# Attention beside a gated feed-forward on one core: zero matmuls at the end, VectorE out of the last 24 banks, and one bank for two chunks' last gate and up tiles

## The chip, the cores and the metric

The kernel runs on one core of a Trainium2 chip. The metric is the time of one execution on the device, in microseconds; shorter is better. Times of the kernel before come from three runs and one further, profiled execution.

## The reference

For one sequence of 2048 rows of 640 numbers in bf16 the kernel computes an attention and a gated feed-forward on the same normalised input, and joins them:

```
xn  = layernorm(x)                                  # x: 2048 x 640
q, k, v = split(xn @ wqkv)                          # 32 heads of 20
s   = concat_h(softmax(q_h @ k_h.T / sqrt(20)) @ v_h) @ wo
h   = sigmoid(xn @ w_gate) * (xn @ w_up)            # 2048 x 1728
g   = silu(h @ w_down)                              # 2048 x 640
out = x + s * g
```

The scores are 32 matrices of 2048 x 2048, and each of their 134 million elements needs an exponential. 1728 is 13 tiles of 128 and one of 64.

## The kernel before, in words

**Setup.** Layer norm, the transposed input xnT and the first keys, queries and values come from an order written out by hand (ORDER). The change leaves it alone.

**Passes and banks.** The queries are cut into four chunks of 512 (qc), the heads into eight groups of four (g); a pass is one (qc, g), so there are 32. In a pass each head has 16 blocks of 128 keys. The scores of one head and one block fill one PSUM bank (128 keys x 512 queries), so a pass has 64 banks and the kernel NB = 2048. Four heads lie in the four row strips of TensorE. The last pass starts at bank LAST = 1984 and is cut into three parts of 256, 128 and 128 queries (PARTS), which end at banks 2016, 2032 and 2048; there a bank holds two or four blocks of keys of a narrower part.

**Who takes the exponential.** The scores go alternately into sets of three banks (sc0) and two banks (sc1). ScalarE turns a whole set into probabilities `p` with one instruction (L1293). VectorE takes single banks on the side, from one of two further PSUM banks ("spare" in the trace, "misc0" and "misc1" in the code): a cut at zero (`dy`, L1313) for each bank, then three polynomial steps for two banks together (`du` L1334, `du` L1338, `p` L1344), each of which may be split into two halves of 512 columns to let other VectorE work in between. `dve_bank` (L1231) decides which bank VectorE may take. TensorE then multiplies the probabilities by the values into the bank `oacc` (L1470, "PV" below). A column of ones in v gives the sum for the softmax.

**The planner.** All this is written by a loop that runs while the program is built. It keeps clocks of its own for TensorE, ScalarE and VectorE, with a cost for each kind of work, and at each step writes a set of scores, a PV batch, a step of some other job, or a zero matmul; so it fixes the order of the instructions on every engine. The other jobs, with due times in banks, are: keys, values and queries of later passes; `gateup_job` (L646) for one chunk and one tile of 128 gate and up columns (five matmuls L664 into one of the two banks, a tanh on ScalarE L671, five matmuls L677 into the other, and a product on VectorE L681 into `hT`); `down_job` (L687, matmuls L700); `out_job`, the output product of a finished chunk; and for the last chunk `part_job` (L758), which does the product of five of the eight head groups ahead, with matmuls L773, a step on VectorE L778 and a DMA that adds x (L781).

**Zero matmuls.** `zero_add` (L1441) writes a matmul with zero weights into `oacc` (L1446) or into a free bank (L1452) where the planner sees a gap, as long as the matmul time that it has counted in the last 3400 ns is under ENOUGH = 2500 ns. Each job step may say how much of its time counts; the matmuls with `pick` count nothing.

**The end.** The last pass but one is normalised on the chip by `near_job` (L834) and each part of the last pass by `last_job` (L895): the accumulator is copied out (`oev`, L794, L885 on VectorE, L887 on ScalarE for the last part), transposed by fp32 matmuls with `pick`, a 128 x 4 matrix that selects the four sums (L839, L912), inverted (`rq`, L846, L918), spread (`rb`, L850, L923), transposed back with a 128 x 128 identity (L857, L940) and multiplied (`oT`, L863, L947). Then follow the last three head groups of the output product (L902), the gate on VectorE (L988 for half a row tile, L970 for the last row tile), the sum (`ot`, L991) and a DMA to the output (L992).

Of the kernel before, what the change touches and what calls it, by code (L numbers as in the profile page):

```python
# [15 lines left out]
P = 128  # L16
PARTS = ((0, 256), (256, 128), (384, 128))
HEAD = 32
GH = 4
# [39 lines left out]
def kernel(  # L59
# [20 lines left out]
    fsz_list = [min(P, F - i * P) for i in range(NFT)]  # L80
    TT = S // P
# [31 lines left out]
    pick = const.tile([P, GH], FP32, name="pick")  # L113
# [62 lines left out]
    with tc.tile_pool(name="setup", bufs=1) as sp, \  # L176
# [181 lines left out]
        nc.gpsimd.memset(pick, 0.0)  # L358
        for j in range(GH):
            nc.gpsimd.memset(pick[32 * j:32 * j + 1, j:j + 1], 1.0)  # L360
# [8 lines left out]
    WINDOW, ENOUGH = 3400.0, 2500.0  # L369
# [274 lines left out]
    hTs, h_cells, d_cells = {}, {}, {}  # L644

    def gateup_job(c, kf):  # L646
        fsz = fsz_list[kf]
        if kf == 0 and c:
            yield "known", lambda: len(d_cells.get(c - 1, [])) == QC // P
        elif kf:  # L650
            yield "known", lambda: c in hTs
        yield "known", lambda: pe[0] > glu_t.get((c, kf), 1e18)
        hT_free = d_cells[c - 1] if c and not kf else []
        n = c * NFT + kf + WB - 1
        if n < NQC * NFT:
            load_glu(n // NFT, n % NFT)
        wg, wu = glu_w.pop((c, kf))
        if kf == 0:
            hTs[c] = glu[0].tile([P, NFT, QC], BF16, tag="hT", bufs=1, name="hT")
        hT = hTs[c]  # L660
        cols = slice(c * QC, (c + 1) * QC)
        held, psg = yield "bank",
        for kd in range(KD):
            nc.tensor.matmul(psg[0:fsz, :], lhsT=wg[:, kd, 0:fsz], rhs=xnT[:, kd, cols],  # L664
                             start=(kd == 0), stop=(kd == KD - 1))
            yield "mm", MM5
        made = {}

        def gate():
            made["t"] = wk.tile([P, QC], BF16, tag="tnh", bufs=2, name="tnh")  # L670
            nc.scalar.activation(out=made["t"][0:fsz, :], in_=psg[0:fsz, :], func=ACT.Tanh, scale=0.5)  # L671

        gated = act.add(480.0, [Cell(pe[0] + PE_OUT + 100.0), *tnh_free[-2:-1]], gate, 0, EXP_LAG)
        give_bank(held, gated)
        held, psu = yield "bank",
        for kd in range(KD):
            nc.tensor.matmul(psu[0:fsz, :], lhsT=wu[:, kd, 0:fsz], rhs=xnT[:, kd, cols],  # L677
                             start=(kd == 0), stop=(kd == KD - 1))
            yield "mm", MM5
        tnh_free.append(dve.add(600.0, [Cell(pe[0] + PE_OUT), gated, *hT_free],  # L680
                                lambda: nc.vector.scalar_tensor_tensor(  # L681
                                    out=hT[0:fsz, kf, :], in0=made["t"][0:fsz, :], scalar=1.0,
                                    in1=psu[0:fsz, :], op0=ALU.add, op1=ALU.mult), 1))
        give_bank(held, tnh_free[-1])
        h_cells.setdefault(c, []).append(tnh_free[-1])

    def down_job(tt):  # L687
# [7 lines left out]
        for h in range(2):  # L695
            e0_, e1_ = h * HALF, (h + 1) * HALF
            held, psd = yield "bank",
            for kf in range(NFT):
                fsz = fsz_list[kf]
                nc.tensor.matmul(psd[:, 0:HALF], lhsT=hT[0:fsz, kf, t4 * P:(t4 + 1) * P],  # L700
                                 rhs=glu[1][0:fsz, kf, e0_:e1_], start=(kf == 0), stop=(kf == NFT - 1))
# [56 lines left out]
    def part_job(t4):  # L758
# [5 lines left out]
        if not ahead:  # L764
            buf = glu[0].tile([P, NFT, QC], BF16, tag="hT", bufs=1, name="hT")
# [68 lines left out]
    def near_job(qc, g):  # L834
# [3 lines left out]
        for k in range(QC // P):  # L838
            nc.tensor.matmul(pd[:, k * GH:(k + 1) * GH], lhsT=oev[:, k * P:(k + 1) * P], rhs=pick,  # L839
                             start=True, stop=True, skip_group_check=True)  # L840
# [54 lines left out]
    def last_job(u):  # L895
# [15 lines left out]
        for k in range(n):  # L911
            nc.tensor.matmul(pd[:, k * GH:(k + 1) * GH], lhsT=part["oev"][:, k * P:(k + 1) * P], rhs=pick,  # L912
                             start=True, stop=True, skip_group_check=True)
            yield "mm", 250.0, 0.0

        def invert():
            made["rq"] = wk.tile([P, n, GH], FP32, tag="den", bufs=2, name="rq")
            nc.vector.reciprocal(out=made["rq"].rearrange("p t j -> p (t j)"), in_=pd[:, 0:GH * n])  # L918
# [86 lines left out]
    PART_DUE = [LAST - 8 + 8 * t4 for t4 in range(4)]  # L1005
# [39 lines left out]
    for c in range(NQC):  # L1045
# [3 lines left out]
        for kf in range(NFT):  # L1049
            jobs.append(Job(gateup_job(c, kf), GU_COST, 0, STAGE_END[c]))  # L1050
# [36 lines left out]
    def load_bulk():  # L1087
        if not glu_from or sum(bulk) == NFT + XT or front() < glu_from[0] + BULK_EVERY * (1 + sum(bulk)):
            return
        if bulk[0] < NFT:  # L1090
            kf = bulk[0]
            fsz = fsz_list[kf]
            nc.sync.dma_start(out=glu[1][0:fsz, kf, :], in_=B_w_down[kf * P:kf * P + fsz, :])
# [347 lines left out]
    def zero_add(room):  # L1441
        if streamed() >= ENOUGH or (0.0 if mode[0] == "fill" else INTO["fill"]) + MM5 > room:
# [164 lines left out]
```

## Time and profile before

| what | value |
|---|---|
| median of three runs | 887.37 us (885.86 to 888.43) |
| the profiled execution's own time | 887.83 us |
| its span, first to last instruction | 885.8 us |
| TensorE busy | 810.3 us (91%) |
| VectorE busy | 849.6 us (96%) |
| ScalarE busy | 864.0 us (98%) |
| mean granted clock of TensorE | 0.993 |

"Busy" is the time in which at least one instruction of the engine was under way. Matmuls overlap each other in the array, so TensorE's share says little by itself. All places in time below count from the first instruction of the span. In rows of the timeline the first number is the start and the second the length, both in microseconds; instructions of one kind that follow each other are merged into one row with their count.

### The profile page before, as it was taken

The numbers are of one execution on the slowest core, as the hardware profiler recorded it, in microseconds if no ns is written. First come the engines' busy times: TensorE is split into PE (matmuls) and PEld (weight loads), VectorE is DVE, ScalarE is ACT, GpSimd is POOL, SyncE is SP. The second block draws the span as 40 slices with busy tenths as digits, with TensorE's granted clock in tenths as the row PEclk, the third lists the DMA queues.
The fourth block names the chain that finished last, engine by engine and source line by source line (L and its number), as shares of the span: only waits on it lengthen the run. The fifth ranks groups of instructions, "written<-read, shape, count | busy, mean of one in ns | idle before, by whom it ended". The sixth has DMA issues, their size and how long they took to land.

```text
span 885.8 us, 16787 instructions
## 1 busy us (share of the span) xinstructions
PE 810.3 (91%) x6380; PEld 295.7 (33%) x6459; DVE 849.6 (96%) x1198; ACT 864.0 (98%) x830; POOL 158.3 (18%) x304
## 2 busy tenths in 40 slices
PE   8999999899998999999999999999999999999896
PEld 3434333332222333232233432232333332233344
DVE  7799999999999999999999999999999999999996
ACT  7999999999999999999999999999999999999994
POOL 8401111110111112111111221110112211111200
PEclk9999999999999999999999999999999999999988
DMA  8212231115542124322321243212222343200120
GB/s 319 59 52 61 73 105 36 50 53 143 154 127 58 35 82 87 56 65 66 80 50 52 80 72 79 66 41 65 54 64 66 94 67 79 64 20 14 29 46 31
DMA packets 107446, 64.10 MB, mean 72 GB/s; under 512 B 80226, under 2 KB 101750, under 8 KB 107274
## 3 DMA queue, kind: packets, MB, share of 16 engines
q1 hardware_dynamic: 97382, 47.21, 20.2%
q0 software_dynamic: 9984, 15.83, 7.9%
q8 instruction: 50, 0.82, 0.4%
q14 instruction: 30, 0.25, 0.1%
HBM read 50.18 MB, written 16.11 MB: 75 GB/s over the span
## 4 chain that ended last, share of the span: by engine, by line
ACT 50%; DVE 18%; issue 16%; PE 13%; DMA 2%; SPq 0%; POOL 0%; DVEq 0%; ACTq 0%; POOLq 0%
ACT p L1293 47%; PE sc L1267 4%; DVE dy L1313 4%; DVE du L1338 3%; DVE du L1334 3%; DVE p L1344 3%; PE work L700 2%; PE oacc L1470 2%; ACT tnh L671 2%; PE work L664 1%; DMA wqd<-in_A_wqkv_dram 1%; DVE hT L681 1%; PE oacc L1446 1%; ACT td L711 1%; PE work L677 1%
## 5 line engine op out<-in xcount | busy, mean ns | idle before, releaser
L1293 ACT ACTIVATE p<-sc 128x1536 bf16<-128x1536 f32 x711 | 818.8, 1341 | 3.2 <-PE sc L1267 1.6
L1267 PE MATMUL sc<-qT,kT_all 21*128 21x512 bf16 (+2 forms) x1889 | 278.9, 371 | 50.3 <-ACT p L1293 44.3
L1313 DVE TENSOR_SCALAR dy<-spare 128x512 f32<-128x512 f32 x271 | 184.7, 682 | 9.2 <-PE spare L1267 6.8
L1267 PEld LDWEIGHTS <-kT_all 21*128 21x128 bf16 x2176 | 90.2, 91 | 287.1 <-issue 274.9
L1334 DVE SCALAR_TENSOR_TENSOR du<-dy 128x1024 f32<-128x1024 uint16 (+1 forms) x163 | 169.0, 1038 | 2.4
L1338 DVE SCALAR_TENSOR_TENSOR du<-du,dy 128x1024 f32<-128x1024 f32 (+1 forms) x156 | 167.5, 1075 | 1.1
L1344 DVE SCALAR_TENSOR_TENSOR p<-du,dy 128x1024 uint16<-128x1024 f32 (+1 forms) x153 | 167.2, 1092 | 0.8
L1470 PE MATMUL oacc<-p,v_all 128*21 128x512 bf16 (+2 forms) x2176 | 158.1, 371 | 1.1 <-issue 0.5
L1267 PE MATMUL spare<-qT,kT_all 21*128 21x512 bf16 (+2 forms) x287 | 103.9, 373 | 1.6 <-DVE hT L681 0.7
L700 PE MATMUL work<-wd,hT 128*128 128x320 bf16 x448 | 80.3, 302 | 0.0
L798 POOL DMA_DIRECT2D den_dram<-oev x30 | 17.5, 583 | 346.9 <-DVE oev L794 307.5
L664 PE MATMUL work<-xnT,wg 128*128 128x512 bf16 (+1 forms) x263 | 75.8, 382 | 3.4 <-DVE dy L1313 1.5
L677 PE MATMUL work<-xnT,wu 128*128 128x512 bf16 (+1 forms) x263 | 73.0, 381 | 2.7 <-DVE dy L1313 0.7
L814 POOL DMA_DIRECT2D rl<-rec_dram x120 | 60.2, 523 | 54.9 <-DMA rec_dram<-den 48.4
L1470 PEld LDWEIGHTS <-v_all 128*21 128x21 bf16 x2176 | 32.2, 90 | 61.2 <-issue 57.7
L1446 PE MATMUL oacc<-xnT,zero 128*128 128x512 bf16 x140 | 48.6, 392 | 2.2 <-issue 2.2
L700 PEld LDWEIGHTS <-hT 128*128 128x128 bf16 x448 | 36.7, 97 | 41.2 <-issue 31.0
L808 POOL DMA_DIRECT2D rec_dram<-den x30 | 16.3, 545 | 134.8 <-DVE den L807 134.8
L671 ACT ACTIVATE tnh<-work 128x512 bf16<-128x512 f32 (+1 forms) x56 | 38.9, 694 | 0.0
L681 DVE SCALAR_TENSOR_TENSOR hT<-tnh,work 128x512 bf16<-128x512 bf16 (+1 forms) x56 | 37.8, 675 | 0.1
L677 PEld LDWEIGHTS <-wu 128*128 128x128 bf16 (+1 forms) x280 | 24.1, 98 | 39.0 <-issue 21.6
L664 PEld LDWEIGHTS <-wg 128*128 128x128 bf16 (+1 forms) x280 | 22.0, 98 | 40.4 <-issue 28.4
(132 smaller groups left out, 578.3 us busy)
## 6 DMA issues: line engine op xcount, KB each, us to landing
wg<-in_B_w_gate_dram SPq DMA_DIRECT2D x52, 160.0 KB
wu<-in_B_w_up_dram SPq DMA_DIRECT2D x52, 160.0 KB
rl<-rec_dram POOLq DMA_DIRECT2D x120, 64.0 KB, 2.4
qT<-q_dram SPq DMA_DIRECT2D x31, 128.0 KB
gq_dram<-d POOLq DMA_DIRECT2D x12, 320.0 KB, 2.5
gqr<-gq_dram SPq DMA_DIRECT2D x12, 320.0 KB
kT_all<-k_dram SPq DMA_DIRECT2D x28, 128.0 KB
wd<-in_B_w_down_dram SPq DMA_DIRECT2D x13, 160.0 KB
```

Source lines behind the costliest of these rows:

```text
L664: nc.tensor.matmul(psg[0:fsz, :], lhsT=wg[:, kd, 0:fsz], rhs=xnT[:, kd, cols], start=(kd == 0), stop=(kd == KD - 1))
L677: nc.tensor.matmul(psu[0:fsz, :], lhsT=wu[:, kd, 0:fsz], rhs=xnT[:, kd, cols], start=(kd == 0), stop=(kd == KD - 1))
L700: nc.tensor.matmul(psd[:, 0:HALF], lhsT=hT[0:fsz, kf, t4 * P:(t4 + 1) * P], rhs=glu[1][0:fsz, kf, e0_:e1_], start=(kf == 0), stop=(kf == N ...
L814: nc.gpsimd.dma_start(out=t["rl"][32 * j:32 * j + 32, :], in_=rec_dram[n, j:j + 1, :].to_broadcast([32, QC]))
L1267: nc.tensor.matmul(ps[:, c0:c0 + n], lhsT=kT_all[rows, g, kt * P:(kt + 1) * P], rhs=qTs[qc, g][rows, q0:q0 + n], start=True, stop=True, ti ...
L1293: nc.scalar.activation(out=buf.tile(), in_=ps, func=ACT.Exp, bias=EXP_BIAS, scale=exp_scale)
L1313: nc.vector.tensor_scalar(out=pair.y[:, i * 512:(i + 1) * 512], in0=ps, scalar1=LEAST, scalar2=None, op0=ALU.max)
L1334: nc.vector.scalar_tensor_tensor(out=t["u"][:, a:e], in0=t["f"][:, a:e], scalar=CUBE_2, in1=t["f"][:, a:e], op0=ALU.add, op1=ALU.mult)
L1338: nc.vector.scalar_tensor_tensor(out=t["u"][:, a:e], in0=t["u"][:, a:e], scalar=CUBE_1, in1=t["f"][:, a:e], op0=ALU.add, op1=ALU.mult)
L1344: nc.vector.scalar_tensor_tensor(out=t["p"][:, a:e], in0=t["u"][:, a:e], scalar=CUBE_SCALE, in1=t["y"][:, a:e], op0=ALU.mult, op1=ALU.add)
L1446: nc.tensor.matmul(oacc, lhsT=zero, rhs=xnT[:, 0, 0:QC], start=not begun, stop=not begun, skip_group_check=True)
L1470: nc.tensor.matmul(oacc[32 * j:32 * j + 1 + Dh, q0:q0 + width], lhsT=v_all[:, kt, GH * g + j, 0:1 + Dh], rhs=buf.ap[:, i, c0:c0 + width], ...
```

## The change

1. **Zeros.** From bank LAST - 16 on, the limit ENOUGH on zero matmuls is lifted: every gap that the planner sees and that is long enough gets one. After the last PV, zeros may fill the wait of the last jobs as well.
2. **The small transposes.** `pick` is gone; the transposes of `oev` use the 128 x 128 identity, and the inversion reads every 32nd column. The planner counts 200 of their 330 ns as matmul time.
3. **VectorE's share.** `dve_bank` gives VectorE none of the banks from NB - 24 on.
4. **Part products.** The `part_job`s of the last chunk are due at LAST - 24, - 16, - 8 and 0 in place of LAST - 8, 0, + 8 and + 16, and a job that waits for an event (`near_job`, `last_job`) goes to the head of the jobs under way.
5. **The 64-wide tiles.** The last gate and up tile has 64 columns. Chunks 0 and 1, and chunks 2 and 3, now do it together: for each of the five steps one matmul for the one chunk into the upper 64 rows of a bank and one for the other chunk into the lower 64, from the two halves of TensorE's columns; then one tanh and one product of 128 rows, into a tile `hE` of its own. The job count of gate and up falls from 56 to 54. The last 64 rows of w_down are loaded twice, so that both halves find them.

From the first shared tile on the planner's order differs: on ScalarE from the 283rd of its 828 instructions, on TensorE from the 4043rd of 12872.

```diff
+    EDGE = fsz_list[-1]
+    assert 2 * EDGE == P
...
-    pick = const.tile([P, GH], FP32, name="pick")
...
-    WINDOW, ENOUGH = 3400.0, 2500.0
+    WINDOW, ENOUGH, ZEROS = 3400.0, 2500.0, 16
...
     def gateup_job(c, kf):
...
+        both = kf == NFT - 1
+        if both:
+            hEs[c] = hEs[c + 1] = glu[0].tile([P, QC], BF16, tag="hE", bufs=1, name="hE")
+            fsz = 2 * EDGE
+        into = hEs[c] if both else hTs[c][:, kf, :]
+
+        def product(ps, w, kd):
+            for k in range(1 + both):
+                nc.tensor.matmul(ps[EDGE * k:EDGE * (k + 1), :] if both else ps, lhsT=w[:, kd, 0:EDGE if both else P],
+                                 rhs=xnT[:, kd, (c + k) * QC:(c + k + 1) * QC], start=(kd == 0), stop=(kd == KD - 1),
+                                 tile_position=(0, EDGE * k), skip_group_check=both)
+
         held, psg = yield "bank",
         for kd in range(KD):
-            nc.tensor.matmul(psg[0:fsz, :], lhsT=wg[:, kd, 0:fsz], rhs=xnT[:, kd, cols],
-                             start=(kd == 0), stop=(kd == KD - 1))
-            yield "mm", MM5
+            product(psg, wg, kd)
+            yield "mm", MM5 + 60.0 * both, MM5
...
     def near_job(qc, g):
...
-            nc.tensor.matmul(pd[:, k * GH:(k + 1) * GH], lhsT=oev[:, k * P:(k + 1) * P], rhs=pick,
+            nc.tensor.matmul(pd[:, k * P:(k + 1) * P], lhsT=oev[:, k * P:(k + 1) * P], rhs=identf,
                              start=True, stop=True, skip_group_check=True)
-            yield "mm", 250.0, 0.0
+            yield "mm", 330.0, 200.0
...
-            nc.vector.reciprocal(out=made["rq"].rearrange("p t j -> p (t j)"), in_=pd[:, 0:GH * QC // P])
+            nc.vector.reciprocal(out=made["rq"].rearrange("p t j -> p (t j)"), in_=pd[:, 0:QC:P // GH])
...
-    PART_DUE = [LAST - 8 + 8 * t4 for t4 in range(4)]
+    PART_DUE = [LAST-24 + 8 * t4 for t4 in range(4)]
...
-        for kf in range(NFT):
+        for kf in range(NFT - c % 2):
             jobs.append(Job(gateup_job(c, kf), GU_COST, 0, STAGE_END[c]))
...
-            flight.insert(0 if x.due >= NB else sum(y.when is not None for y in flight), x)
+            flight.insert(0, x)
...
     def dve_bank(banks):
         b = min((x for x in coming(GH) if x not in banks), default=None)
         if b is None:
+            return None
+        if b >= NB - 24:
             return None
...
     def zero_add(room):
-        if streamed() >= ENOUGH or (0.0 if mode[0] == "fill" else INTO["fill"]) + MM5 > room:
+        if streamed() >= (ENOUGH if at_bank[0] < LAST - ZEROS else 1e9) or (0.0 if mode[0] == "fill" else INTO["fill"]) + MM5 > room:
             return False
...
-    take_part(len(PARTS) - 1, pe[0])
+    oacc_free[0] = take_part(len(PARTS) - 1, pe[0])
     while flight or jobs or timed or act.queue or dve.queue:
         advance(pe[0])
         if not fill(len(steps) - 1):
-            pe[0] += 50.0
+            waits = [c.t for j in flight if j.asks and j.asks[0] == "wait" for c in j.asks[1]]
+            if not (flight or jobs) or None in waits or not zero_add(max(waits, default=1e18) - pe[0]):
+                pe[0] += 50.0
```

How many instructions of each kind the program has, before and after: exponentials on ScalarE 711 and 711, of the same sizes; tanh 56 and 54; `dy` on VectorE 271 and 271; products of gate and up on VectorE 56 and 54; polynomial steps in VectorE's queue 472 and 486, since the planner splits more of them into halves; zero matmuls in `oacc` 183 and 193.

More of the change, by code (lines that the diff above doesn't have):

```diff
@@ L911, in last_job @@
         for k in range(n):
-            nc.tensor.matmul(pd[:, k * GH:(k + 1) * GH], lhsT=part["oev"][:, k * P:(k + 1) * P], rhs=pick,
+            nc.tensor.matmul(pd[:, k * P:(k + 1) * P], lhsT=part["oev"][:, k * P:(k + 1) * P], rhs=identf,
                              start=True, stop=True, skip_group_check=True)
-            yield "mm", 250.0, 0.0
+            yield "mm", 330.0, 200.0
         def invert():
             made["rq"] = wk.tile([P, n, GH], FP32, tag="den", bufs=2, name="rq")
-            nc.vector.reciprocal(out=made["rq"].rearrange("p t j -> p (t j)"), in_=pd[:, 0:GH * n])
+            nc.vector.reciprocal(out=made["rq"].rearrange("p t j -> p (t j)"), in_=pd[:, 0:n * P:P // GH])
         def spread():
@@ L1092, in load_bulk @@
             fsz = fsz_list[kf]
-            nc.sync.dma_start(out=glu[1][0:fsz, kf, :], in_=B_w_down[kf * P:kf * P + fsz, :])
+            for r in range(0, P, fsz):
+                nc.sync.dma_start(out=glu[1][r:r + fsz, kf, :], in_=B_w_down[kf * P:kf * P + fsz, :])
             bulk[0] += 1
```

35 lines of the change are left out of this document (16 added, 19 removed).

## Prediction

> **What bounds the kernel now.** I read the chain of waits on the page first, then the costliest groups, then the busy time by windows, and last the timeline of the end.
>
> ```profile
> ACT 50%; DVE 18%; issue 16%; PE 13%; DMA 2%; SPq 0%; POOL 0%; DVEq 0%; ACTq 0%; POOLq 0%
> ...
> L1293 ACT ACTIVATE p<-sc 128x1536 bf16<-128x1536 f32 x711 | 818.8, 1341 | 3.2 <-PE sc L1267 1.6
> L1267 PE MATMUL sc<-qT,kT_all 21*128 21x512 bf16 (+2 forms) x1889 | 278.9, 371 | 50.3 <-ACT p L1293 44.3
> ```
>
> Half of the chain is ScalarE (ACT), nearly all of it the exponentials of L1293. Of TensorE's idle time ahead of scores, 44.3 us is spent waiting for ScalarE; the reverse wait is 1.6 us. So in the long middle TensorE has room, and only what takes time from ScalarE, or makes it wait, moves the end. In the windows below the first numbers are the stretch and its length, then busy time and instructions of PE, PEld, DVE, ACT and POOL, then the granted clock, the DMA share and GB/s.
>
> ```profile
> 58.00:860.00 802.00, 741.08 (x5674) 259.81 (x5744) 785.34 (x1057) 799.40 (x746) 131.23 (x238) 1.00 0.28 68
> 846.64:850.06 3.42, 2.88 (x25) 0.94 (x25) 3.42 (x5) 3.42 (x5) 0.00 (x0) 1.00 0.09 20
> 853.47:856.88 3.41, 3.15 (x51) 2.04 (x45) 3.38 (x5) 3.41 (x4) 0.00 (x0) 1.00 0.38 87
> 856.88:860.30 3.42, 3.22 (x43) 1.23 (x45) 3.42 (x6) 3.38 (x4) 0.00 (x0) 0.50 0.00 0
> 860.30:863.71 3.41, 3.08 (x32) 2.09 (x25) 2.16 (x3) 2.52 (x3) 0.00 (x0) 0.50 0.00 0
> ```
>
> From 58 to 860 us ScalarE rests 802.00 - 799.40 = 2.6 us. The end is different: from 856.88 to 863.71 TensorE has half its clock, and ScalarE is busy for only 2.52 of the last 3.41 us of it. The timeline of ScalarE's end, and of TensorE where ScalarE waits:
>
> ```profile
> 859.33 1.02 ACT L1293 ACTIVATE p<-sc 128x1024 bf16<-128x1024 f32 x1
> 860.88 2.53 ACT L1293 ACTIVATE p<-sc 128x1536 bf16<-128x1536 f32 x2 [0.53 <-PE spare L1267]
> 864.46 10.06 ACT L1293 ACTIVATE p<-sc 128x1536 bf16<-128x1536 f32 x9 [1.05 <-PE sc L1267]
> 875.23 0.28 ACT L887 ACTIVATE oev<-oacc 128x128 f32<-128x128 f32 x1 [0.71 <-PE oacc L1470]
> ```
> ```profile
> 862.60 1.37 PE L857 MATMUL work<-identf,rb 128*128 128x128 f32 x6
> 863.90 0.42 PE L1267 MATMUL sc<-qT,kT_all 21*128 21x128 bf16 x12
> ```
>
> Two stalls of 0.53 and 1.05 us, and between them and the last exponential nothing: 22 banks in 10.06 us, 0.457 us a bank. The longer stall ends with scores that stand in TensorE's queue behind six fp32 records (two for each matmul of the program), which take 1.37 us at half clock. After the last exponential (874.52) come 11.3 us in which ScalarE has one instruction. So the end has three parts: ScalarE's work, its stalls at half clock, and the closing chain.
>
> **The change part by part.**
>
> *ScalarE's work.* The exponentials stay 711, of the same sizes. Two tanh go.
>
> ```profile
> 634.01 0.66 ACT L671 ACTIVATE tnh<-work 64x512 bf16<-64x512 f32 x1
> 634.49 2.43 ACT L1293 ACTIVATE p<-sc 128x1536 bf16<-128x1536 f32 x2
> ```
>
> A tanh of 64 rows holds ScalarE for 634.49 - 634.01 = 0.48 us. Two of them: **-0.96 us**, on the engine that sets the end. Bounds: 2 x 0.66 = 1.32 at most; at least 0, if the planner's new order makes ScalarE rest that much longer.
>
> *VectorE.* Two products of gate and up go, and 14 polynomial steps more are halves.
>
> ```profile
> 849.12 1.21 DVE L1344 SCALAR_TENSOR_TENSOR p<-du,dy 128x1024 uint16<-128x1024 f32 x1
> 850.25 0.68 DVE L1313 TENSOR_SCALAR dy<-spare 128x512 f32<-128x512 f32 x1
> 850.86 0.48 DVE L778 SCALAR_TENSOR_TENSOR hT<-work,kT_all 128x320 f32<-128x320 f32 x1
> ```
>
> Start to start, 1024 columns take 1.13 us and 512 take 0.61, so a split costs 2 x 0.61 - 1.13 = 0.09 us: 14 x 0.09 = 1.3 against 2 x 0.61 = 1.2 saved. I take zero. VectorE takes 271 banks as before; within them three in place of four lie in the last part of the queries. That one bank costs ScalarE 0.46 us at the end and spares it as much earlier; while ScalarE has no rest, the place is the same to it.
>
> *The shared 64-wide tiles on TensorE.* 40 matmuls of 512 columns become 20 pairs.
>
> ```profile
> 839.64 0.61 PE L1470 MATMUL oacc<-p,v_all 128*21 128x512 bf16 x8 [0.25 <-issue]
> 856.40 0.38 PE L1446 MATMUL oacc<-xnT,zero 128*128 128x512 bf16 x1 [0.16 <-issue]
> 868.57 0.60 PE L1446 MATMUL oacc<-xnT,zero 128*128 128x512 bf16 x2
> ```
>
> A second matmul of 512 columns adds 0.60 - 0.38 = 0.22 us. Eight PV matmuls take only 0.61 us: two groups of four, side by side in strips of 32 columns. No row shows two strips of 64; the nearest is PV. If a pair goes side by side it takes 0.22 us and 20 of them save 4.4 us of TensorE; if one after the other, nothing is saved and each pair takes 0.43 us where the planner counts 0.276, 20 x 0.154 = 3.1 us too late in all. I take side by side. The 44.3 us of waiting for ScalarE cover either; without that cover the 3.1 us would go to ScalarE. The added DMA (64 rows of w_down) and four loads fewer on SP's queue I cost at nothing: the tile is needed only at the first down product, and the planner lets 4 us pass after the last of these loads.
>
> *Transposes with the identity.* Four columns become 128, and fp32.
>
> ```profile
> 854.42 0.61 PE L839 MATMUL work<-pick,oev 128*128 128x4 f32 x4
> 869.91 0.61 PE L940 MATMUL work<-identf,rb 128*128 128x128 f32 x4
> ...
> 853.47:856.88 3.41, 1.22 (x8) 1.04 (x8) 1.00 0.38 87
> ```
>
> Four records take 0.61 us with `pick` and 0.61 us with the identity, so their time is unchanged. What changes is what they do for the clock. The last row is L839 alone in the window before the clock fell: 1.22 of its 3.15 busy us are matmuls of four columns. The window at 846.64 is less busy (2.88 us), without such matmuls, and the clock stayed. So the clock follows the columns sent, not the time that a record is open. Counting 0.21 us for 512 columns and four strips as one, I get 1.1 us for 853.47 and 1.5 us for 846.64; the fall lies between. In the new order the eight records there send 128 columns, the near job starts five banks earlier, and the thinnest stretch that I find, banks 2018 to 2029, has 2.1 us of columns in ten ScalarE banks (4.6 us), 1.6 us in 3.41. I therefore expect the full clock to hold. Then the 1.05 us stall goes, whose cause is in the rows: **-1.05 us**. In the new order two of the four transposes also stand behind a set of scores. The stall of 0.53 us I leave standing as a bound.
>
> [...]
>
> *Zeros.* In the order there are 22 from bank 1968 on, 23 before. Each costs TensorE 0.22 us, or twice that at half clock, ahead of whatever the planner did not foresee. The rows 868.57 show two of them while ScalarE ran on without a rest. I cost them at nothing; bound + 0.5 us for one or two that land before late scores.
>
> *The closing chain.* Before, two PV batches and two out-products stand after the last scores; then:
>
> ```profile
> 874.55 0.63 PE L1470 MATMUL oacc<-p,v_all 128*21 128x128 bf16 x32
> 875.11 0.99 PE L902 MATMUL work<-wo_pad,oT 128*128 128x320 bf16 x6
> 878.52 0.43 PE L902 MATMUL outs<-wo_pad,oT 128*128 128x320 bf16 x2
> ...
> 876.25 0.18 DVE L918 RECIPROCAL rq<-side 128x4 f32<-128x4 f32 x1
> 876.47 0.23 DVE L923 COPY rb<-rq 128x128 f32<-128x128 f32 x1
> 877.04 0.83 DVE L991 TENSOR_TENSOR ot<-kT_all,hT 128x640 bf16<-128x640 f32 x1 [0.34 <-PE work L940]
> 877.78 0.28 DVE L947 TENSOR_TENSOR oT<-oev,work 128x128 bf16<-128x128 f32 x1
> 878.18 0.48 DVE L988 SCALAR_TENSOR_TENSOR kT_all<-work,kT_all 128x320 f32<-128x320 f32 x1
> 879.44 0.82 DVE L970 SCALAR_TENSOR_TENSOR kT_all<-outs,kT_all 128x640 f32<-128x640 f32 x1
> 881.82 0.82 DVE L991 TENSOR_TENSOR ot<-kT_all,hT 128x640 bf16<-128x640 f32 x1
> ```
>
> From the first `rq` to the last `ot` VectorE has 12 instructions here and 881.82 - 876.25 = 5.57 us. In the new order the second part is finished before the last scores' exponentials, since its scores no longer wait for VectorE, and only seven remain: rq, rb, ot, oT, ot, gate, ot. Counted from the end of the last PV (874.55 + 0.63 = 875.18 before): three out-matmuls end at 0.51, the last half gate starts at 0.55 and is 0.48 us long, `rq` starts at 1.03 (1.07 before), `rb` at 1.25, `ot` at 1.48, `oT` 0.74 later at 2.22, the second `ot` at 2.50, the gate at 3.24 (its `outs` end at 2.22 + 0.28 + 0.43 = 2.93), the last `ot` 0.82 after it at 4.06. Before, it starts at 881.82 - 875.18 = 6.64. So **-2.58 us**. It is less if half gates of the second part come late as well: one more of them and its `ot` in this chain cost 0.48 + 0.74 us, which leaves -1.4. What follows the last `ot` stays 885.80 - 881.82 us.
>
> Sum: 0.96 + 1.05 + 2.58 = 4.59 us. The profiled execution took 887.83 us, of which the span is 885.8 and 2.0 lie around it: 883.2. It lies 0.46 us above the median of the runs, 887.37, so for the median 882.8.
>
> **The rivals.**
>
> *The clock falls again (0.20).* [...] For it: I know two windows on either side of the limit, not the limit. Then the stalls stay, and 0.96 + 2.58 = 3.54 us remain: 883.8.
>
> *The middle gives it back (0.13).* The pairs go one after the other and the 3.1 us land on ScalarE, or the new order, different for two thirds of the run, makes ScalarE rest 5.7 us where it was 2.6. Against: VectorE's load is the same and TensorE's no larger. 887.37 - 4.59 + 3.1: 885.9.
>
> *The end runs at half clock throughout, and TensorE becomes its bound: slower (0.05).* From bank 2000 on ScalarE has 44 banks, 20.1 us. TensorE's columns there, by the count above, take 13.1 us, ten zeros and 14 transposes with 128 columns among them. Each us at half clock does half a us of it, so TensorE binds from 14 us at half clock on, twice the 6.83 us of before; over the whole stretch it needs 26.2 us, 6.1 more than ScalarE: 887.37 - 3.54 + 6.1 = 889.9. Against: before, the clock came back by itself at 863.71 with the same kind of work.
>
> *The zeros do nothing.* Their count hardly moves, 22 for 23; then the clock hangs on the transposes alone, which is in the first rival's chance.
>
> **How the numbers follow.** The forecast has 0.62, at 882.8. A change under 0.3% (2.7 us) can't be told from none here. Faster by more: nearly all of the forecast, most of the first rival and little of the second, 0.60 + 0.16 + 0.02 = 0.78. Slower: the third rival and an ill-fated middle, 0.07. Same: 0.15. Range: below, the 0.53 us stall and half of the 2.6 us of rest go too, 882.8 - 1.8 = 881.0; above, the second rival, 886.0 rounded up. Outside lie the slower case and the outer ends.
>
> **What would show it.** Right: the granted clock 1.00 in every window from 850 us to the last PV; no ScalarE wait over 0.3 us there; 11 to 12 us from the last exponential to the end of the span become 8 to 9; pairs of shared matmuls starting within some ns of each other. Wrong: a clock of 0.50 before the last PV, ScalarE's rest in the middle well above 2.6 us, or more than seven VectorE instructions after the last `rq`.

## The result, and the profile after

The changed kernel takes 884.68 us (median of 21 executions, 883.16 to 887.23), the kernel before, on the same chip, 887.84 us (21 executions, 885.34 to 896.11). The ratio is 0.9956, with a 95% interval of 0.9938 to 0.9973: faster by 0.44%; the two medians lie 3.2 us apart. Executions of one kernel differ among themselves, and they differ with TensorE's mean granted clock; the profiled execution of the changed kernel, 887.23 us with a span of 885.3 us and a clock of 0.996, is the slowest of its 21. So I read it first for its places and come to the sizes below.

The page of the changed kernel, its chain of waits and two of its costliest groups:

```profile
ACT 52%; issue 17%; DVE 17%; PE 9%; DMA 2%; POOL 1%; SPq 0%; DVEq 0%; ACTq 0%; POOLq 0%
...
L1305 ACT ACTIVATE p<-sc 128x1536 bf16<-128x1536 f32 x711 | 818.9, 1344 | 5.7 <-PE sc L1279 3.2
L1279 PE MATMUL sc<-qT,kT_all 21*128 21x512 bf16 (+2 forms) x1892 | 278.5, 370 | 51.7 <-ACT p L1305 46.6
```

ScalarE still carries the chain, TensorE's share of it has gone from 13% to 9%, and ScalarE's idle time ahead of exponentials has grown from 3.2 to 5.7 us. The windows say where it rests:

```profile
58.00:860.00 802.00, 736.88 (x5648) 257.49 (x5720) 783.19 (x1069) 795.51 (x741) 131.71 (x238) 1.00 0.27 68
...
854.00:858.00 4.00, 3.36 (x44) 2.02 (x44) 3.91 (x6) 4.00 (x5) 0.85 (x1) 1.00 0.22 44
858.00:862.00 4.00, 3.65 (x57) 2.17 (x54) 4.00 (x7) 4.00 (x4) 0.00 (x0) 1.00 0.18 42
862.00:866.00 4.00, 3.44 (x75) 2.17 (x70) 3.97 (x6) 4.00 (x5) 0.00 (x0) 1.00 0.00 0
```

From 854 us on the clock is 1.00 and ScalarE is busy for 4.00 of every 4.00 us: the half clock of before and its two stalls are gone. But over the long middle ScalarE rests 802.00 - 795.51 = 6.5 us, where it rested 2.6 us. The timeline of ScalarE's end, and of the two TensorE rows that answer to it:

```profile
839.73 37.23 ACT L1305 ACTIVATE p<-sc 128x1536 bf16<-128x1536 f32 x33
877.86 0.28 ACT L896 ACTIVATE oev<-oacc 128x128 f32<-128x128 f32 x1 [0.90 <-PE oacc L1482]
```
```profile
855.17 0.94 PE L848 MATMUL work<-identf,oev 128*128 128x128 f32 x6
...
877.18 0.63 PE L1482 MATMUL oacc<-p,v_all 128*21 128x128 bf16 x32
```

The last 33 exponentials run in one row of 37.23 us without a wait long enough to be listed; they end at 876.96, and the span at 885.3, 8.34 us later (11.28 before). VectorE's closing chain:

```profile
878.76 0.17 DVE L927 RECIPROCAL rq<-side 128x4 f32<-128x4 f32 x1
878.97 0.23 DVE L932 COPY rb<-rq 128x128 f32<-128x128 f32 x1
879.11 0.82 DVE L1000 TENSOR_TENSOR ot<-kT_all,hT 128x640 bf16<-128x640 f32 x1
879.85 0.29 DVE L956 TENSOR_TENSOR oT<-oev,side 128x128 bf16<-128x128 f32 x1
880.05 0.82 DVE L1000 TENSOR_TENSOR ot<-kT_all,hT 128x640 bf16<-128x640 f32 x1
880.79 0.82 DVE L979 SCALAR_TENSOR_TENSOR kT_all<-outs,kT_all 128x640 f32<-128x640 f32 x1
881.64 0.82 DVE L1000 TENSOR_TENSOR ot<-kT_all,hT 128x640 bf16<-128x640 f32 x1
```

Seven instructions from `rq` to the last `ot`, the seven that the prediction lists. The last `ot` starts 881.64 - 877.81 = 3.83 us after the last PV, where 4.06 was forecast and 6.64 was before.

Something new stands at 291 us, just behind the first shared tile: windows first, then ScalarE.

```profile
287.65:291.06 3.41, 3.41 (x31) 0.99 (x31) 3.31 (x4) 3.41 (x4) 0.00 (x0) 1.00 0.22 56
291.06:294.48 3.42, 2.41 (x21) 0.83 (x20) 3.35 (x5) 3.42 (x5) 0.00 (x0) 1.00 0.00 0
294.48:297.89 3.41, 3.15 (x15) 1.07 (x19) 3.38 (x6) 2.33 (x3) 1.15 (x2) 0.50 0.02 2
297.89:301.30 3.41, 3.41 (x21) 1.09 (x13) 0.88 (x1) 2.39 (x2) 0.00 (x0) 0.50 0.04 2
```
```profile
297.81 1.02 ACT L1305 ACTIVATE p<-sc 128x1024 bf16<-128x1024 f32 x1 [1.08 <-PE sc L1279]
299.32 1.45 ACT L1305 ACTIVATE p<-sc 128x1536 bf16<-128x1536 f32 x1 [0.49 <-PE sc L1279]
301.68 2.40 ACT L1305 ACTIVATE p<-sc 128x1024 bf16<-128x1024 f32 x2 [0.91 <-PE spare L1279]
```

The window at 291.06 is thin, the next two have half the clock, and ScalarE waits 1.08 + 0.49 + 0.91 us there. It is a stall at half clock like the one that the end has lost, in another place.

### The profile page after: what moved, and what is told of

The parts are those of the page before. It is cut to its first block, busy times and chain, and to the rows that moved or that the text cites. A ratio compares the mean times of both kernels' runs of the same rounds, so it can differ in the third digit from the quotient of the medians.

```text
span 885.3 us, 16801 instructions
## 1 busy us (share of the span) xinstructions
PE 806.4 (91%) x6388; PEld 293.1 (33%) x6469; DVE 849.1 (96%) x1210; ACT 864.1 (98%) x828; POOL 158.4 (18%) x299
## 4 chain that ended last, share of the span: by engine, by line
ACT 52%; issue 17%; DVE 17%; PE 9%; DMA 2%; POOL 1%; SPq 0%; DVEq 0%; ACTq 0%; POOLq 0%
ACT p L1305 49%; DVE dy L1325 4%; DVE p L1356 3%; DVE du L1350 3%; DVE du L1346 3%; PE sc L1279 3%; ACT tnh L679 2%; PE work L709 2%; PE oacc L1482 2%; DMA den<-den_dram 1%; PE work L667 1%; DMA x_sb<-in_A_x_dram 1%; DVE d L713 1%; DVE stats L261 1%; DVE oT L835 1%
## 5 line engine op out<-in xcount | busy, mean ns | idle before, releaser
L667 PE MATMUL work<-xnT,wg 128*128 128x512 bf16 (+1 forms) x262 | 73.3, 382 | 3.7 <-DVE dy L1325 1.0
L709 PE MATMUL work<-wd,hT 128*128 128x320 bf16 x416 | 74.7, 306 | 1.6 <-DVE dy L1325 0.9
L667 PE MATMUL work<-xnT,wu 128*128 128x512 bf16 (+1 forms) x265 | 70.7, 381 | 2.9 <-DVE dy L1325 1.2
L1458 PE MATMUL oacc<-xnT,zero 128*128 128x512 bf16 x147 | 50.9, 386 | 2.8 <-issue 2.5
L709 PEld LDWEIGHTS <-hT 128*128 128x128 bf16 x416 | 34.6, 99 | 37.2 <-issue 26.5
L679 ACT ACTIVATE tnh<-work 128x512 bf16<-128x512 f32 x54 | 37.6, 696 | 0.0
L688 DVE SCALAR_TENSOR_TENSOR hT<-tnh,work 128x512 bf16<-128x512 bf16 x52 | 35.3, 678 | 0.3 <-ACT tnh L679 0.2
L748 PE MATMUL work<-wo_pad,oT 128*128 128x320 bf16 x192 | 34.3, 301 | 0.8 <-DVE dy L1325 0.5
```

The costliest lines, as they stand in the source:

```text
L667: nc.tensor.matmul(ps[EDGE * k:EDGE * (k + 1), :] if both else ps, lhsT=w[:, kd, 0:EDGE if both else P], rhs=xnT[:, kd, (c + k) * QC:(c + ...
L709: nc.tensor.matmul(psd[:, 0:HALF], lhsT=h_in[rows, t4 * P:(t4 + 1) * P], rhs=glu[1][rows, kf, e0_:e1_], start=(kf == 0), stop=(kf == NFT - 1))
L1458: nc.tensor.matmul(oacc, lhsT=zero, rhs=xnT[:, 0, 0:QC], start=not begun, stop=not begun, skip_group_check=True)
```

## The experiments

**The time against the clock.** My theory was that TensorE's clock sets what the executions differ in; the rival, that their spread has nothing to do with it. Nothing is edited here: the changed kernel runs again, twice, with profiles of their own.

> The changed kernel as it is, to see how its executions spread and where the clock falls. Theory A (the forecast, corrected): without a fall of the clock in the middle the gain is the full 4.6 us of the three terms, about 0.9948 of before; each stretch of 6.8 us at half clock, such as the one at 294 us of the profiled execution, gives 2 to 3 us of it back, so that executions with a mean clock of 0.996 are 2 to 3 us longer than those with 0.999 or more. Rival: the spread has nothing to do with the clock, and executions of the same mean clock lie 2 us or more apart.

> The changed kernel once more, on the chip of the two others, to compare with them: 0.995 of before, as twice before.

Measured: 884.04 us (883.28 to 885.31) at a ratio of 0.9947 [0.9923, 0.9972], and 885.15 us (883.4 to 887.48) at 0.9955 [0.9933, 0.9977]. The clock fell at 294.35 for 3.41 us in the first profile (mean clock 0.997), and in the second at 294.46 and at 731.37 (0.996). The theory holds: the changed kernel's 17 executions with a mean clock of 0.999 have a median of 883.7 us, the four with 0.996 one of 886.3. Each execution comes with its mean granted clock, so all of them can be sorted by it; this table holds every kernel of the study.

| kernel | executions | median, us | of them at a clock of 0.998 or more | their median, us |
|---|---|---|---|---|
| before | 94 | 888.6 | 18 | 886.1 |
| changed | 41 | 884.7 | 27 | 883.9 |
| parts 1 to 4 alone | 12 | 886.3 | 11 | 886.2 |
| part 5 alone | 12 | 886.4 | 2 | 884.5 |
| changed, with `pick` | 12 | 891.5 | 1 | 883.7 |
| before, with the identity | 12 | 886.4 | 8 | 886.2 |
| changed, zeros limited | 12 | 884.9 | 8 | 884.1 |
| changed, VectorE not limited | 12 | 885.3 | 6 | 884.7 |
| changed, ENOUGH 2700 | 12 | 885.9 | 6 | 885.3 |
| parts 1 to 4, NB - 32 | 12 | 886.6 | 6 | 885.2 |
| changed, surcharge 20 | 12 | 885.4 | 7 | 884.3 |

The row of before gathers its executions beside all these runs, on three chips, where its medians are 888.3, 889.4 and 888.5 us. The identity in the kernel before, the zeros limited, VectorE not limited and ENOUGH 2700 ran on the second, without the changed kernel beside them; so differences of under a microsecond between their rows and the changed kernel's say little. At the same, nearly full clock the change gains 886.1 - 883.9 = 2.2 us. Away from it before loses 888.6 - 886.1 = 2.5 us in the median and the changed kernel 0.8: by this sorting 1.7 us of gain come from the clock falling less often. Together 3.9, the difference of the medians in the table. The split is an estimate, since the mean clock also counts the half clock at the very end, where TensorE has no matmul left: 5.0 us of it in the profile of before (from 880.78 us on, with 0.00 us of matmuls), 0.3 to 1.9 us in those of the changed kernel. An execution of before can thus lie under 0.998 without a fall ahead of that; its eight at 0.997 have a median of 886.3. So the medians of the last column can be compared, the counts ahead of them less well.

**Each half of the change alone.** First the end without the shared tiles: the edits of parts 1 to 4 on the kernel before.

```diff
-    pick = const.tile([P, GH], FP32, name="pick")
+    WINDOW, ENOUGH, ZEROS = 3400.0, 2500.0, 16
+    PART_DUE = [LAST-24 + 8 * t4 for t4 in range(4)]
+        if b >= NB - 24:
+            return None
...
```

> Parts 1 to 4 of the change (zeros, transposes with the identity, VectorE's limit, due times) on the kernel before; the 64-wide tiles stay apart. In its order nine VectorE instructions stand after the last rq, against eleven before and six in the changed kernel. Theory A: the stall at half clock goes (-1.05 us), the closing chain gains only some 0.5 us, no tanh goes: -1.5 us, 0.998 of before; no fall of the clock near 290 us. Rival (the end's edits carry the gain by themselves): -3.6 us, 0.996.

Measured: 886.26 us (885.1 to 889.48), ratio 0.9977 [0.9961, 0.9993]. The last eleven VectorE instructions, of which the first and the last row:

```profile
878.97 0.18 DVE L914 RECIPROCAL rq<-side 128x4 f32<-128x4 f32 x1
...
882.34 2.28 DVE L987 TENSOR_TENSOR ot<-kT_all,hT 128x640 bf16<-128x640 f32 x3
```

Three `ot` of 640 columns stand at the end, and 10.7 us lie between the last exponential and the end of the span: the closing chain is hardly shorter than before. At full clock this kernel gains nothing (886.2 against 886.1); its 2.2 us in the median are all clock. And the clock can fall without shared tiles: in its profile it does so at 722.4, in the middle, for 6.83 us.

Then the shared tiles alone: part 5 on the kernel before.

```diff
+        both = kf == NFT - 1
+                                 tile_position=(0, EDGE * k), skip_group_check=both)
...
-        for kf in range(NFT):
+        for kf in range(NFT - c % 2):
```

> Part 5 alone (the shared 64-wide tiles) on the kernel before; the end keeps pick, the limit on zeros and VectorE's share. Seven VectorE instructions stand after the last rq in its order, so the closing chain is shorter though none of the end's edits is in. Theory A: tanh -0.96 us and closing chain -1 to -2 us, the stall at half clock may stay: -2 to -3 us, 0.997 of before, with the same fall of the clock near 291 us as the changed kernel in part of the executions. Rival (the shared tile brings only its two tanh): -1 us, 0.999.

Measured: 886.4 us (883.47 to 891.27), ratio 0.9977 [0.9953, 1.0]. The clock still falls at the end (855.42 in its profile), so only two of twelve executions are near full clock; those two have a median of 884.5. Its closing stretch is 8.6 us, with nine VectorE instructions from the last `rq` on, although nothing of the end was edited: the new order alone put the last sets elsewhere.

**The small transposes.** The same order on every engine, and only the width of the transposes differs: the changed kernel with `pick` put back, the planner's costs kept.

```diff
-            nc.tensor.matmul(pd[:, k * P:(k + 1) * P], lhsT=oev[:, k * P:(k + 1) * P], rhs=identf,
+            nc.tensor.matmul(pd[:, k * GH:(k + 1) * GH], lhsT=oev[:, k * P:(k + 1) * P], rhs=pick,
```

> The changed kernel with the 128 x 4 pick in the eight transposes of oev, everything else and the order of all engines the same. Theory A (the clock follows the columns sent): 128 columns less in each of 16 records, 14 of them in the last 32 us; the clock falls to 0.50 somewhere between 853 and 875 us in most executions, ScalarE stalls 1 us or more there, and the time is 1 to 1.5 us above the changed kernel's. Rival (the time a matmul is open counts, or the zeros alone hold the clock): clock 1.00 up to the last PV and no difference to the changed kernel above 0.3 us.

Measured: 891.5 us (883.7 to 895.4), 6.8 us more than the changed kernel's 884.7 where 1 to 1.5 were expected, ratio to before 1.0024 [0.9996, 1.0053]. Its windows at the end; the second row is the transposes alone, with what reads and writes `oev`:

```profile
849.69:853.10 3.41, 2.89 (x30) 1.88 (x30) 3.41 (x6) 3.41 (x4) 0.85 (x1) 1.00 0.01 2
849.69:853.10 3.41, 1.22 (x8) 1.04 (x8) 0.44 (x1) 0.00 (x0) 0.00 (x0) 1.00 0.01 2
853.10:856.51 3.41, 2.98 (x42) 1.11 (x42) 3.17 (x5) 3.39 (x4) 0.00 (x0) 0.50 0.45 101
...
862.00:866.00 4.00, 4.00 (x63) 2.45 (x60) 1.26 (x2) 3.09 (x3) 0.00 (x0) 0.50 0.00 0
866.00:870.00 4.00, 3.67 (x42) 2.38 (x36) 3.38 (x8) 3.83 (x4) 0.00 (x0) 0.50 0.02 4
870.00:874.00 4.00, 4.00 (x68) 2.69 (x67) 2.92 (x5) 1.96 (x2) 0.00 (x0) 0.50 0.00 0
```

The window ahead of the fall is 2.89 of 3.41 us busy, but 1.22 us of that are eight records of four columns. From 853.10 on the clock stays at one half, nine windows or 30.72 us, to 883.82; over the whole span the mean clock is 0.982. ScalarE waits again and again, and the last accumulator comes late too:

```profile
862.14 1.45 ACT L1309 ACTIVATE p<-sc 128x1536 bf16<-128x1536 f32 x1 [1.79 <-PE sc L1283]
...
874.10 3.28 ACT L1309 ACTIVATE p<-sc 128x1024 bf16<-128x1024 f32 x3 [1.20 <-PE sc L1283]
...
884.30 0.28 ACT L900 ACTIVATE oev<-oacc 128x128 f32<-128x128 f32 x1 [2.12 <-PE oacc L1486]
```

The one execution in which the clock held (0.999) took 883.7 us, as the changed kernel does. So the four columns cost nothing as work, and about 7 us through the clock.

The same edit the other way round, the identity in the kernel before, in its own order:

```diff
-            nc.tensor.matmul(pd[:, k * GH:(k + 1) * GH], lhsT=oev[:, k * P:(k + 1) * P], rhs=pick,
+            nc.tensor.matmul(pd[:, k * P:(k + 1) * P], lhsT=oev[:, k * P:(k + 1) * P], rhs=identf,
```

> The kernel before with the 128 x 128 identity in place of pick in the eight transposes of oev; planner's costs and so the order of all engines as before. Theory A (the columns of these transposes decide on the clock at the end): the clock stays at 1.00 near 857 us in most executions, both stalls of ScalarE there go, and the closing chain stays at 11.3 us: the time comes to that of the executions before with a mean clock of 0.998 or more, 885.4 to 887 us, 2 us or more below the median of before. Rival (the order around it decides): no difference to before, 1.000.

Measured: 886.36 us (884.79 to 889.6) against 889.36 beside it, ratio 0.9973 [0.9952, 0.9995]. Windows and ScalarE's end:

```profile
858.00:862.00 4.00, 3.45 (x60) 2.42 (x63) 3.67 (x5) 4.00 (x5) 0.00 (x0) 1.00 0.00 0
862.00:866.00 4.00, 3.18 (x93) 2.27 (x87) 3.65 (x7) 4.00 (x4) 0.00 (x0) 1.00 0.01 4
```
```profile
838.76 32.98 ACT L1289 ACTIVATE p<-sc 128x1536 bf16<-128x1536 f32 x29
872.45 0.28 ACT L883 ACTIVATE oev<-oacc 128x128 f32<-128x128 f32 x1 [0.71 <-PE oacc L1466]
```

The clock is full, the last 29 exponentials run without a listed wait, and they end at 871.74 us (874.52 before). The closing stretch is as long as before, 883.1 - 871.74 = 11.4 us. At full clock this kernel gains nothing (886.2 against 886.1), as it should if only the clock is held. It also has the median of parts 1 to 4 together, 886.4 to 886.3, so of those four parts the transposes are the one whose worth can be seen alone.

**The zeros.** The changed kernel with the limit kept to the end, which is six zeros fewer:

```diff
-        if streamed() >= (ENOUGH if at_bank[0] < LAST - ZEROS else 1e9) or (0.0 if mode[0] == "fill" else INTO["fill"]) + MM5 > room:
+        if streamed() >= ENOUGH or (0.0 if mode[0] == "fill" else INTO["fill"]) + MM5 > room:
```

> The changed kernel with the limit on zeros kept through the last pass: six zeros fewer, the same closing chain. Theory A (the transposes hold the clock, zeros add nothing): within 0.5 us of the changed kernel, no more falls of the clock at the end than there. Rival (zeros in the gaps of the last pass hold the clock): falls to 0.50 after 850 us in a good part of the executions, and a median 1 us or more above the changed kernel's.

Measured: 884.93 us (883.3 to 891.31), ratio 0.9965 [0.9945, 0.9986], the same closing stretch of 8.35 us and a fall of the clock in the same place, at 294.87 (mean clock 0.997). The lifted limit can't be told from nothing. The other way, more zeros throughout, in the hope of holding the clock in the middle:

```diff
-    WINDOW, ENOUGH, ZEROS = 3400.0, 2500.0, 16
+    WINDOW, ENOUGH, ZEROS = 3400.0, 2700.0, 16
```

> The changed kernel with ENOUGH 2700 in place of 2500: 80 zeros more in the whole run. Theory A (what is left of the spread is falls of the clock in the middle, as at 294 us): no execution with a mean clock under 0.998, the spread of the executions shrinks, and the median falls by 0.5 us against the changed kernel. Rival (the zeros stand in front of scores): each of the added zeros that lands late costs ScalarE 0.1 to 0.2 us, and the median rises by 1 us or more.

Measured: 885.91 us (884.76 to 888.04), ratio 0.9974 [0.9959, 0.999]. The profile shows no fall before the end, but the mean clocks of the other executions go down to 0.993, and at full clock it is at 885.3, above the changed kernel's 883.9; beside before, too, its ratio is the worse one, 0.9974 for 0.9947 to 0.9956. Eighty zeros more (278 for 198 in all) do not buy the clock in every execution and cost over a microsecond; VectorE also gets three banks fewer (268), so that cost isn't the zeros' alone.

**VectorE's last banks.** The changed kernel without the limit, and parts 1 to 4 with a longer one:

```diff
-        if b >= NB - 24:
-            return None
```

> The changed kernel without VectorE's limit: it may take banks up to the end again. In its order nine VectorE instructions stand after the last rq in place of six. Theory A (the closing chain is what stands after the last rq, and VectorE's banks matter only through that): the stretch from the last exponential to the end grows from 8.3 to 9.5 us, the median by 1 to 1.5 us, clock as in the changed kernel. Rival (VectorE's late banks hold up the last PV): the last exponentials' probabilities wait for VectorE's and the median grows by 2.5 us or more.

```diff
-        if b >= NB - 24:
+        if b >= NB - 32:
```

> Parts 1 to 4 without the shared tiles, as in the run of the end alone, with VectorE's limit at the last 32 banks in place of 24: six instructions stand after the last rq, and VectorE takes 268 banks, three fewer than before. Theory A (the gain is the clock at the end plus the length of the closing chain; the shared tiles cost the middle about 2 us and save one): closing stretch 8.3 us in place of 10.7, middle as in the kernel before, three banks more on ScalarE +1.4 us: 0.5 to 1.5 us below the run of the end alone, so about the changed kernel's time without its shared tiles. Rival (the shared tiles are part of the gain): 1 us or more above the changed kernel.

Measured: 885.33 us (884.29 to 888.09), ratio 0.9961 [0.994, 0.9982], without the limit; and 886.63 us (884.92 to 888.86), 0.9986 [0.9971, 1.0001], with the longer one. Without it ten VectorE instructions stand from the last `rq` on and the closing stretch is 9.95 us for 8.34. The median shows 0.6 of these 1.6 us and the time at full clock 0.8, less than the 1 to 1.5 expected. With NB - 32 parts 1 to 4 come down from eleven to seven, of which the first and the last:

```profile
877.76 0.17 DVE L914 RECIPROCAL rq<-side 128x4 f32<-128x4 f32 x1
...
880.64 0.83 DVE L987 TENSOR_TENSOR ot<-kT_all,hT 128x640 bf16<-128x640 f32 x1
```

Its closing stretch is 8.65 us for 10.7, but of these 2 us the time at full clock shows 886.2 - 885.2 = 1.0, and the median none, since fewer of its executions keep the clock (6 of 12 for 11 of 12). It also gives VectorE two banks fewer than NB - 24 does (268 for 270), which at 0.457 us a bank is some 0.9 us more for ScalarE, an estimate. So the limit shortens the chain, but how far it has to reach depends on where the order puts the last sets.

**The planner's price of a pair.** The planner adds 60 ns to a shared pair; with 20 ns it lays the middle out again.

```diff
-            yield "mm", MM5 + 60.0 * both, MM5
+            yield "mm", MM5 + 20.0 * both, MM5
```

> The changed kernel with the planner's surcharge for a pair of shared matmuls at 20 ns in place of 60 (a pair takes 212 to 216 ns in the trace). The order is planned anew from the first pair on: eight zeros more, five VectorE instructions after the last rq, 269 banks on VectorE. Theory A (the middle's loss of 2 us belongs to one particular order and not to the shared tiles as such): ScalarE's loss from 320 to 850 us differs from the changed kernel's by 1 us or more in either direction. Rival (the shared tiles themselves make ScalarE wait): the loss stays within 0.5 us of the changed kernel's.

Measured: 885.39 us (883.66 to 889.16), ratio 0.9966 [0.9948, 0.9985]; at full clock 884.3. To compare middles I add up, over ScalarE's instructions from 320 to 850 us, how much later the next one starts than is usual for its form: 9.0 us before, 11.0 in the second profile of the changed kernel, 11.0 here. So the price of the pairs doesn't show as what makes the middle dearer. That the loss stays is what the rival expected, by which the shared tiles themselves make ScalarE wait; but one profile doesn't settle it. The order of ENOUGH 2700, a third one with shared tiles, has 10.0, and other profiles without a fall in that stretch give 10.2 to 11.2 for the changed kernel's order, and 8.6 (with the identity) and 10.4 (NB - 32, the same order there up to 841 us) for the one of before.

## Why the prediction was right, and where it was not

It said 882.8 us, 881.0 to 886.0, with 0.78 for faster by over 0.3%. Measured are 884.68 us and 0.44% faster: the direction is right and the time lies in the range, 1.9 us above the point. That it does is in part luck: the middle gave back some 3.7 us, which the sum had at nothing, and the stalls and the closing chain brought 1.4 us more than forecast. One of the signs named for being wrong, a rest in the middle well above 2.6 us, came true. Its terms one by one, the span of the second profile of the changed kernel (883.38 us) against that of before (885.80):

*ScalarE's work, forecast -0.96.* The tanh are gone and the gain is given back: the prediction's lower bound, "at least 0, if the planner's new order makes ScalarE rest that much longer", is what happened, and it went past it. From 320 to 850 us ScalarE loses 11.0 us in place of 9.0 by the count above, 1.9 more before rounding; by the other profiles named there some 1.5 to 2 us is a fair reading. From 58 to 320 us it loses another 1.8 us more, nearly all of it by the fall at 294.35: in the profile with `pick`, of the same order and at full clock there, it is 0.3. Part of the 1.9 us are waits too short to be listed. One that is listed, ScalarE and TensorE in the second profile:

```profile
732.19 1.02 ACT L1305 ACTIVATE p<-sc 128x1024 bf16<-128x1024 f32 x1 [0.73 <-PE spare L1279]
```
```profile
730.52 1.24 PE L667 MATMUL work<-xnT,wg 128*128 128x512 bf16 x5 [0.63 <-DVE dy L1325]
```

Five gate matmuls wait 0.63 us for a bank that VectorE's `dy` still holds; the scores stand behind them in TensorE's queue, and ScalarE waits 0.73 us for those. This is the second rival's result, by the second of the two mechanisms that it named, the new order, and by a fall of the clock that it did not name. Its 5.7 us of rest compare with 6.5 and, in the second profile, 802.00 - 797.01 = 5.0 us. It was given 0.13, and an order that differs from ScalarE's 283rd instruction on deserved more. Whether the 1.9 us belong to the shared tiles as such or to one of the planner's choices was not settled; with the surcharge at 20 ns the loss was the same.

*The pairs.* Right: side by side. The row and the two groups of all pairs:

```profile
290.11 1.03 PE L667 MATMUL work<-xnT,wu 128*64 128x512 bf16 x8
```
```profile
L667 PE MATMUL work<-xnT,wg 128*64 128x512 bf16 x20 | 3.1, 391 | 0.0
L667 PE MATMUL work<-xnT,wu 128*64 128x512 bf16 x20 | 2.9, 386 | 0.0
```

Eight matmuls of 512 columns take 1.03 us; one after the other they would take 0.38 + 7 x 0.22 = 1.9, an estimate from the prediction's rows of one and of two zero matmuls. The two of a pair start 3 or 4 ns apart, and pairs in a row follow at 0.215 or 0.216 us. But narrow matmuls side by side also send fewer columns by the prediction's own count, and the prediction did not look at what that does to the clock: the window at 291.06 holds the first shared tile's last pair and then gaps, 2.41 us busy in all, and the clock falls to 0.50 behind it. With `pick` the same stretch of the same order is as thin (2.38 us busy from 291.06 to 294.48) and the clock holds; why it does there is not shown. That is the first rival's event, the clock falling again, in a place that I had not searched; my search for the thinnest stretch covered the end alone.

*The stall at half clock, forecast -1.05.* The mechanism was right for these kernels and is shown, not only argued: with the order fixed, the profiles with four columns have half clock near the end, 6.83 us before and 30.72 us in the changed kernel with `pick`, and those with 128 have 1.00 there (both kernels with exchanged transposes). The size was too small. Both stalls went, 0.53 and 1.05 us, and from 850 us to the last exponential ScalarE's loss fell from 2.43 to 0.37 us, by 2.1. The term was priced from one execution with 6.83 us of half clock; over many executions the falls cost before 2.5 us in the median, and the new order with `pick` loses 6.8. Nor does the busy time explain the fall with `pick`: the clock fell behind a window that was 2.89 us of 3.41 busy, and only the columns differed from a kernel in which it held.

*Zeros at nothing.* Right: 884.93 us with the limit, 884.7 without. That they do nothing, the last rival, is what the runs show for the lifted limit at the end.

*The closing chain, forecast -2.58.* It measured 11.28 - 8.34 = 2.94 us, by the seven instructions listed. The reason that I gave for it, that the second part is finished early "since its scores no longer wait for VectorE", is half of it: without the limit three instructions more come late (9.95 us), but the limit on the order of before (parts 1 to 4) leaves eleven, and there it takes NB - 32 to come to seven and 8.65 us. The shared tiles alone, without any limit, have nine and 8.6 us. So it is how the order of the last sets falls out, which the limit and the shared tiles both move.

*Half clock throughout, the slower rival.* It did not come in the changed kernel. The version with `pick` shows that it was no phantom: 30.72 us at half clock, past the 14 us from which the prediction let TensorE bind, and 891.5 us, near the 889.9 worked out for it. The identity is what kept the changed kernel from it.

The sum, term by term for the two spans: tanh -0.96, 58 to 320 us with the fall at 294 +1.8, the rest of the middle +1.9, the stalls -2.1, the closing chain -2.9, and some -0.2 ahead of the first exponential, together -2.5 against a measured -2.42.

## What to carry to other kernels

Where executions of one kernel scatter, sort them by TensorE's mean granted clock before comparing medians: a change can win by doing less, or by letting the clock fall less often (2.2 and 1.7 us here, an estimate from the table), and the two are found in different columns of it. A matmul that is only four columns wide took as long here as one of 128, 0.61 us for four records of either; the wide form was free (886.2 us for 886.1 at full clock, in the kernel before) and held the clock at the end, where the lifted limit on zeros changed nothing that could be measured. An edit that makes a planner lay out two thirds of the run anew is not a local one: search the whole new order for its thinnest stretch, not only the place that the edit is meant for.

## What the runs showed of the hardware

The granted clock was 1.00 or 0.50 in these traces, and the measured distances between its changes are close to whole multiples of 3.413 us. In the profile of before it falls at 856.88, comes back at 863.71 and falls again at 880.78, after 6.83 and 17.07 us, two and five times that length; in the profile of the changed kernel the places are 294.48, 301.30 and 884.98, after 6.83 and 583.68 us, two and 171 times; and with `pick` it is low for 30.72 us, nine times. For each stretch of 3.41 us on this grid between 60 and 870 us of the first two profiles I count the columns sent, nearly as the prediction does. 512 columns count 0.216 us, which is what most such matmuls in a row take from start to start; strips and pairs side by side count once; and fp32 counts twice, since the two records of one matmul of 128 columns start some 0.11 us apart, where a quarter of 0.216 is 0.054. The two falls then stand behind 1.11 us (853.47, before) and 1.30 us (291.06, changed), and the thinnest windows that start and end at full clock and are followed by it have 1.51 us (174.22) and 1.40 us (103.33). Records of matmuls are missing, though: the trace of before has 183 + 5 weight loads of zeros and 140 + 5 of their matmuls, that of the changed kernel 193 + 5 and 147 + 5. With the missing zeros put in from the loads the falls stand behind 1.32 (where the prediction has 1.1) and 1.30 us, and the thinnest windows without a fall have 1.51 and 1.57. With `pick` the window ahead of the fall, 849.69 to 853.10, has 0.94 us by the rows of its timeline. These counts are estimates, since a matmul at a window's edge is counted to one side.

I had not expected that half clock might hold itself down. In the version with `pick` TensorE is busy for 4.00 of 4.00 us from 862 to 866 and again from 870 to 874, and the clock stays at one half; at half clock it takes about twice as long for its columns (before, a second zero matmul adds 1.03 - 0.63 = 0.40 us there, 0.22 at full clock). That the low clock itself keeps the columns of a window few is my reading; no run tests it. With the missing zeros put in, a window of 1.51 us at half clock was followed by a return of the clock in the profile of before (860.30) and by none in that of the changed kernel (294.48), so what decides the return is not settled.
